# The first two units' queries go from their sums straight into the rows of the max products, and a cleared tile goes

## The chip, the cores and the metric

The kernel runs on one NeuronCore of a Trainium2 chip. The core has five engines, each with a queue of its own that it works through in order: TensorE (PE in the profile; its weight loads are PEld), VectorE (DVE), ScalarE (ACT), GpSimd (POOL) and SyncE (SP), which here only issues transfers. The metric is the device time of one execution in microseconds (us); lower is better.

## The reference

One transformer layer, in float32: 2048 rows of 512, 32 heads of 16 with one shared key and value head, and a GELU MLP of width 1376. The vector `c` gives six rows that shift, scale and gate both halves.

```python
mod = (silu(c) @ w_mod).reshape(1, 6, 1, -1)
sa, ca, ga, sb, cb, gb = (mod[:, i] for i in range(6))
h = layernorm(x) * (1 + ca) + sa
q, k, v = heads(h @ wq), h @ wk, h @ wv
p = softmax(q @ k.T * 16 ** -0.5)
x = x + ga * ((p @ v) @ wo)
h = layernorm(x) * (1 + cb) + sb
x = x + gb * (gelu(h @ w1 + b1) @ w2 + b2)
```

## The kernel before

**Numbers in two parts.** A product is made of three matmuls: each operand is split into a rounded high part and a low part (what the rounding left), and high x high, low x high and high x low are summed in PSUM. `split` makes the two parts, one instruction for each.

**Units.** Attention is made in 64 units: 8 blocks of 256 rows (`HQ`) times 8 groups of four heads. A unit's queries lie in one of four tiles `qst` (`qbufs`), 128 partitions x 2 x 256. In each half of 64 partitions, rows 0 to 15 hold the low part of a head's queries, 16 to 47 the high part twice, and 48 and 49 the row maxima in two parts. `ks` holds the keys in the matching order, with -1 in the rows of the maxima, so one matmul over 64 partitions gives the score minus the maximum. Each unit needs its **max products** first (m, line 517: 32 matmuls, each with one reduction on VectorE, line 522), then its maxima are turned and sent into rows 48 and 49 (`put_max`, line 538), and then come the **score products** (e, 597), the exponentials on ScalarE (p, 598) and the **value products** (acc, 609).

**Queries through DRAM.** `qproj` (before the loop) and `qproj_late` (in the loop) make the queries of 512 rows for a group of two units' heads; `send_q` (413) writes both parts to DRAM, and `load_q` (475) reads them back in the layout of `qst`, four transfers for each of the first four units, six for later ones. The projection for rows 0 to 511 of group 0 serves units 0 and 1, and units 8 and 9.

**Ahead of the loop** the order of every engine's queue is written out by hand. `tc.manual_schedule` keeps each engine's instructions in program order. From line 1259: statistics and normalisation of block 0 of 512 rows (`stats1`, `xhat1`), preparation of the key weights and of the first 128 columns of wq (`prep_wkv`, `prep_wq(0)`), the rows of the modulation (`mod_rows`, `mods`), transposes and scaling of block 0 (`turn1`, `mod1`), and then the first query group, its trip through DRAM for units 0 and 1, the keys and values of block 0, the statistics of blocks 2 and 3 with `heads(1)` among them, and both blocks' normalisation on ScalarE. Then a table, `SLOTS` (line 25), gives the rest: in each slot so many max products (`chunk`), and then named steps, such as "keys 1" (one contraction step of the keys and values of block 1, three matmuls; the last step also copies them out with `kv_out`), "low 1" and "k 1" (the low part of these keys, and its copy for the second half of partitions), "heads 2" (transposes, scaling and splitting of one column block of row block 2), "v 1" (turning the values), "q 1" (a step of the second query group), "wq 1" (weights of a query group), "load" (`load_q` of unit 2) and "rows" (the four late modulation rows). `FIRST_MAX` gives the order of the first 64 max products: units 0 and 1 on each block of 512 keys; the 17th and 18th are the first on block 1. In all 56 max products stand ahead of the loop, two of them in the `while` behind the slots.

Transposes, value transposes, and later the score products share three PSUM banks in turn (`ebank`, e0 to e2); max products have three banks of their own.

**The loop** has 256 bodies, four for each unit. A body makes 8 max products, 8 score products and the 32 value products, and takes one batch of other matmuls if a job offers one, each matmul as two halves over 64 partitions. The jobs in order are the late query projections, the late modulation, more projections, and then the rest of each block (output projection and MLP). A projection is 12 matmuls; `Q_SIZES` cuts it into two batches of 6, or, from job number `Q_LIGHT` on, three of 4. One body in four clock steps; `later(n, fn)` emits a step n clock steps on. Beside that, one step of the weights' preparation stands at the end of a body (`prep_w1`, then `prep_wo`, then `prep_w2`, lines 1082 to 1152): SP loads a piece, and POOL works on it two steps later. `heed` and `wait_early` (462, 467) put the wait for a query transfer on a value product a few clock steps after its issue.

In `prep_w2` the last of 11 pieces has 96 rows of 128; POOL clears the whole tile ahead of its load (1137).

Of the kernel before, what the change touches and what calls it, by code (L numbers as in the profile page):

```python
# [14 lines left out]
P = 128  # L15
# [9 lines left out]
SLOTS = ((4, "keys 1", "keys 1"), (2, "keys 1", "keys 1"), (2, "low 1", "heads 2"), (2, "heads 2", "k 1"), (2, "heads 2"), (2, "heads 2", "v 0"),  # L25
# [10 lines left out]
Q_LIGHT = 12  # L36
# [16 lines left out]
def adaln_mqa_mlp(  # L53
# [282 lines left out]

    hts = {}
# [18 lines left out]
    def xhat1(b, eng):  # L356
# [3 lines left out]
        for t in range(QT):  # L360
# [25 lines left out]

    def kv_out(b):
        ps = kps[b]
        cols = slice(b * BQ, (b + 1) * BQ)
        vt = pro.tile([P, BQ], F32, name=f"vt{b}", tag="vt", bufs=2)  # L390
        for r in range(2):
            nc.scalar.copy(ks[64 * r:64 * r + 48, cols], ps[64 * r:64 * r + 48, :])
        nc.scalar.copy(vt[32:64, :], ps[32:64, :])
        vts[b] = vt

    def low_k(b):
        cols = slice(b * BQ, (b + 1) * BQ)
        nc.vector.tensor_tensor(out=ks[32:48, cols], in0=kps.pop(b)[32:48, :], in1=raw(ks[32:48, cols]), op=ALU.subtract)

# [31 lines left out]
    def qproj(b, g):  # L431

        ps = psum.tile([P, BQ], F32, name=f"qps{b}_{g}", tag="v" if g else "x")
        yield from mm3(ps, qpairs(b, g), 3, 1)
        qH, qL = qtiles(b, g)
        if g == 0:
            nc.scalar.copy(qH, ps)
            nc.vector.tensor_tensor(out=qL, in0=ps, in1=raw(qH), op=ALU.subtract)
        else:
            q32 = pro.tile([P, BQ], F32, name=f"q32_{b}_{g}", tag="h32", bufs=4)  # L440
            nc.scalar.copy(q32, ps)
            split(qH, qL, q32, act, pool)
# [686 lines left out]
    def prep_w2():  # L1129
# [3 lines left out]
        def load(f):  # L1133
            fw = min(P, F - f * P)
            wf = wfs[f] = rp.tile([P, D], F32, name=f"w2f{f}", tag="wf", bufs=3)
            if fw < P:
                nc.gpsimd.memset(wf, 0.0)
            nc.sync.dma_start(out=wf[:fw], in_=w2[f * P:f * P + fw, :])

        def work(f):  # L1140
# [3 lines left out]
            nc.gpsimd.tensor_tensor(out=wfs[f], in0=wfs[f], in1=gb, op=ALU.mult)  # L1144
            split(w2s[g][0][:, f % KD, :], w2s[g][1][:, f % KD, :], wfs[f], nc.gpsimd, nc.gpsimd)
# [65 lines left out]
    projections = [qproj(b, g) for b in range(2) for g in range(KD)]  # L1211
# [50 lines left out]
    prep_wq(0)  # L1262
# [5 lines left out]
    mods()  # L1268
    turn1(0, 2)
# [233 lines left out]
```

## Time and profile before

| | us |
|---|---|
| median of three runs | 1587.57 |
| lowest and highest | 1587.23, 1592.81 |
| the profiled execution's own time | 1589.15 |
| its span, first to last instruction | 1587.3 |

| engine | busy, us | share of the span |
|---|---|---|
| PE | 1562.7 | 98% |
| DVE | 1406.0 | 89% |
| ACT | 1204.3 | 76% |
| POOL | 692.8 | 44% |

A line of a group or of the order of time has the start and the length in us, the engine and line, the operation, what it writes and reads, the shape, how many instructions were merged (x), and in brackets the engine's idle time before it with what ended it, as far as the profile can tell. Matmuls are pipelined, so the lengths of two in sequence overlap; the pace is read from start to start. A line of a window has each engine's busy time and its count of instructions in that stretch, then the granted TensorE clock (PEclk, 1.00 is full), the busy share of the DMA engines and GB/s.

### The profile page before, as it was taken

Reading aid. Unit: us, or ns where it says so; the run is one execution under the profiler, and the core shown is the slowest. Engines: PE = TensorE matmul, PEld = TensorE weight load, DVE = VectorE, ACT = ScalarE, POOL = GpSimd, SP = SyncE. Lnnn points to the kernel's source line nnn. Section 1 sums busy time; section 2 is a strip of 40 time slices with the busy share of each in tenths; the row PEclk is TensorE's granted clock in tenths of the full one; section 3 lists DMA queues with packets and bytes.
Section 4 is the critical chain, followed back from the end, with each engine's and each line's share of the span. In section 5 each row is a group of like instructions: output and inputs, shape, how many; then the busy total and the mean of one; then the engine's idle time right before and its main releaser. Section 6 shows DMA issues by size and latency. Waiting matters only on the chain.

```text
span 1587.3 us, 43409 instructions
## 1 busy us (share of the span) xinstructions
PE 1562.7 (98%) x17491; PEld 1043.9 (66%) x17491; DVE 1406.0 (89%) x2491; ACT 1204.3 (76%) x2417; POOL 692.8 (44%) x1242
## 2 busy tenths in 40 slices
PE   5999999999999999999999999999999999999999
PEld 3556655567766676666766676666766677676667
DVE  6889999899999998999999999999999999999715
ACT  5477777778877887778877887778877788778853
POOL 4345447446513472345622464334712465324721
PEclk8899999999999999999999999999999999999999
DMA  7135423312012120212112130212112130121231
GB/s 263 67 108 177 141 70 101 100 33 97 32 56 67 56 86 23 90 35 94 46 40 86 44 99 19 70 54 86 56 32 92 35 108 22 60 72 50 94 139 68
DMA packets 81022, 121.74 MB, mean 77 GB/s; under 512 B 15966, under 2 KB 55646, under 8 KB 80564
## 3 DMA queue, kind: packets, MB, share of 16 engines
q1 hardware_dynamic: 80804, 118.95, 22.6%
q8 instruction: 137, 2.24, 0.6%
q14 instruction: 65, 0.53, 0.1%
q10 hardware_dynamic: 16, 0.00, 0.0%
HBM read 91.13 MB, written 27.27 MB: 75 GB/s over the span
## 4 chain that ended last, share of the span: by engine, by line
PE 94%; ACT 3%; DVE 1%; DMA 1%; issue 0%; SPq 0%; POOL 0%; DVEq 0%; ACTq 0%
PE acc L609 32%; PE e L597 19%; PE m L517 19%; PE w1ps L193 8%; PE w2ps L193 6%; PE wops L193 3%; PE qps L193 2%; ACT p L598 2%; PE w2ps L187 2%; PE w1ps L187 1%; DVE mx L522 1%; PE tp L193 1%; PE kps L164 1%; PE tp L371 0%; PE modr L289 0%; DMA wm<-in_w_mod_dram 0%
## 5 line engine op out<-in xcount | busy, mean ns | idle before, releaser
L522 DVE TENSOR_REDUCE mx<-m 128x1 f32<-128x512 f32 x2048 | 1271.6, 681 | 105.6 <-PE m L517 95.6
L598 ACT ACTIVATE p<-e 128x512 f32<-128x512 f32 x2048 | 1066.6, 601 | 290.5 <-PE e L597 198.9
L517 PE MATMUL m<-ks,qst 64*128 64x512 f32 x2048 | 829.4, 433 | 6.4 <-DVE ve L205 4.9
L597 PE MATMUL e<-qst,ks 64*128 64x512 f32 x2048 | 729.5, 411 | 2.0 <-ACT wqH L334 1.3
L609 PE MATMUL acc<-p,va 128*32 128x256 f32 x8192 | 550.2, 385 | 1.7 <-DMA qst<-dq 1.7
L517 PEld LDWEIGHTS m<-ks,qst 64*128 64x128 f32 x2048 | 367.4, 184 | 104.6 <-DVE mx L522 85.7
L597 PEld LDWEIGHTS e<-qst,ks 64*128 64x128 f32 x2048 | 356.9, 184 | 112.6 <-ACT p L598 102.6
L609 PEld LDWEIGHTS acc<-p,va 128*32 128x32 f32 x8192 | 214.6, 109 | 219.6 <-issue 113.3
L193 PE MATMUL w1ps<-h2H,w1t 64*128 64x256 f32 x1232 | 236.6, 288 | 0.0
L193 PEld LDWEIGHTS w1ps<-h2H,w1t 64*128 64x128 f32 x1232 | 184.0, 185 | 31.7 <-issue 22.2
L566 POOL TENSOR_SCALAR mt<-turned 8x32 f32<-8x32 f32 x256 | 53.5, 209 | 342.7 <-DVE turned L572 330.6
L193 PE MATMUL w1ps<-h2L,w1t 64*128 64x256 f32 x616 | 169.5, 275 | 0.0
L193 PE MATMUL w2ps<-w2H,gH 64*128 64x256 f32 (+1 forms) x546 | 161.0, 295 | 0.0
L193 PE MATMUL w2ps<-w2H,gL 64*128 64x256 f32 (+1 forms) x546 | 153.9, 282 | 0.0
L193 PE MATMUL w2ps<-w2L,gH 64*128 64x256 f32 (+1 forms) x546 | 153.4, 281 | 0.0
L193 PEld LDWEIGHTS w1ps<-h2L,w1t 64*128 64x128 f32 x616 | 113.7, 185 | 0.0
L193 PEld LDWEIGHTS w2ps<-w2H,gH 64*128 64x128 f32 x546 | 100.5, 184 | 11.7 <-issue 5.4
L193 PEld LDWEIGHTS w2ps<-w2H,gL 64*128 64x128 f32 x546 | 100.7, 184 | 1.7
L193 PEld LDWEIGHTS w2ps<-w2L,gH 64*128 64x128 f32 x546 | 100.7, 184 | 1.3
L949 POOL TENSOR_SCALAR tt<-tt 128x256 f32<-128x256 f32 x77 | 31.2, 406 | 143.8 <-ACT tt L948 143.8
L193 PE MATMUL wops<-woH,onH 64*128 64x256 f32 x224 | 67.9, 303 | 0.0
L193 PE MATMUL wops<-woL,onH 64*128 64x256 f32 x224 | 62.2, 278 | 0.0
(220 smaller groups left out, 1613.1 us busy)
## 6 DMA issues: line engine op xcount, KB each, us to landing
w1t<-dw SPq DMA_DIRECT2D x82, 512.0 KB
qst<-dq SPq DMA_DIRECT2D x128, 64.0 KB
do<-oc SPq DMA_DIRECT2D x64, 128.0 KB
dw<-w1s SPq DMA_DIRECT2D x11, 512.0 KB
xt<-in_A_x_dram SPq DMA_DIRECT2D x4, 1024.0 KB
dq<-qH SPq DMA_DIRECT2D x16, 256.0 KB
dq<-qL SPq DMA_DIRECT2D x16, 256.0 KB
qst<-dq SPq DMA_DIRECT2D x128, 32.0 KB
```

The lines of the kernel that those rows point to most:

```text
L164: nc.tensor.matmul(ps, a, b_, start=begin and n == 0, stop=end and n == last)
L187: nc.tensor.matmul(ps, a, b_, start=first_, stop=last_)
L193: nc.tensor.matmul(ps, a[rows], b_[rows], start=first_ and s == 0, stop=last_ and s == 1)
L517: nc.tensor.matmul(m, qsts[u][rows, j, t * P:(t + 1) * P], ks[rows, kc * 512:(kc + 1) * 512], start=True, stop=True)
L522: nc.vector.tensor_reduce(out=self.mx[u][:, i, kc:kc + 1], in_=m, axis=AX.X, op=ALU.max)
L566: nc.gpsimd.tensor_scalar(out=mt[:, g:g + 32], in0=turned[g:g + 4 * T, :], scalar1=1.0, scalar2=0.0, op0=ALU.mult, op1=ALU.add)
L597: nc.tensor.matmul(e, ks[rows, kt * P:(kt + 1) * P], rhs, start=True, stop=True)
L598: nc.scalar.activation(ptiles[u, K][:, j, s, :], e, AF.Exp, scale=0.25)
L609: ins = nc.tensor.matmul(accs[u][32 * cidx:32 * cidx + 32, :], va[:, kt, :], rhs, start=kt == 0, stop=kt == NKT - 1)
L949: nc.gpsimd.tensor_scalar(out=tt, in0=tt, scalar1=1.0, scalar2=1.0, op0=ALU.mult, op1=ALU.add)
```

## The change

Unit 0's and unit 1's queries no longer go through DRAM ahead of the loop. `prep_w0(u)` makes a weight of 128 columns for each j (two per unit), with the 16 columns of a head repeated three times and 16 columns of zeros, in high and low part: eight parts in all for both units on ScalarE and POOL. `first_queries(u, k)` sums with it into a PSUM bank in the layout of `qst` itself, 24 matmuls of 256 columns for a unit; `queries_out` copies the bank into `qst` (ScalarE), and `low_queries` writes the low part over 16 rows of each half (VectorE). `first_keys` interleaves the keys of block 0 with unit 0's queries, and `low_keys` makes both halves' low parts from PSUM. Unit 0's first two max products stand among unit 1's query products; two and four more follow before `stats1(3)`, and the slots hold 48 instead of 54, so 56 stand ahead of the loop as before. The tail of block 1's normalisation (tiles 2 and 3) is moved to VectorE. The statistics of block 3 come after the eight first max products, where they came ahead of all of them.

The projection of group 0 for rows 0 to 511 becomes the first job of the loop (units 8 and 9 need it), so `prep_wq(0)` moves to a slot near the end, with "wq 2" and "wq 3"; `Q_LIGHT` becomes 14.

In `prep_w2` the tile of the last piece isn't cleared ahead of its load; POOL works on its 96 rows alone, and clears rows 96 to 127 of both parts after that.

```diff
-SLOTS = ((4, "keys 1", "keys 1"), (2, "keys 1", "keys 1"), (2, "low 1", "heads 2"), (2, "heads 2", "k 1"), (2, "heads 2"), (2, "heads 2", "v 0"),
-         (2, "heads 3"), (2, "heads 3"), (2, "heads 3"), (2, "heads 3"), (0, "keys 2"), (2, "keys 2"), (2, "keys 2"), (2, "keys 2"),
-         (2, "low 2", "k 2", "v 1", "wq 1"), (0, "keys 3"), (2, "keys 3"), (2, "keys 3"), (2, "keys 3"), (2, "low 3", "k 3"),
+SLOTS = ((2, "keys 1", "keys 1"), (2, "keys 1", "keys 1"), (2, "low 1", "heads 2"), (2, "heads 2", "k 1"), (2, "heads 2"), (2, "heads 2", "v 0"),
+         (2, "heads 3"), (2, "heads 3"), (2, "heads 3"), (2, "heads 3"), (0, "keys 2"), (1, "keys 2"), (1, "keys 2"), (1, "keys 2"),
+         (1, "low 2", "k 2", "v 1", "wq 1"), (0, "keys 3"), (2, "keys 3"), (2, "keys 3"), (2, "keys 3"), (2, "low 3", "k 3"),
          (0, "v 2"), (2, "q 1"), (2, "q 1"), (2, "q 1"),
-         (2, "q 1", "rows"), (2, "v 3", "load", "wq 2", "wq 3"), (2, "rows"), (2, "rows"), (2, "rows"))
+         (2, "q 1", "rows"), (2, "v 3", "load", "wq 0", "wq 2", "wq 3"), (2, "rows"), (2, "rows"), (2, "rows"))
...
-Q_LIGHT = 12
+Q_LIGHT = 14
+    def prep_w0(u):
+        if u:
+            place_w0(u)
+        for j in range(2):
+            for s in range(2):
+                at = 64 * u + 32 * s + 16 * j
+                w = wqf[:, :, at:at + 16].unsqueeze(2).to_broadcast([P, KD, 3, 16])
+                dh, dl = (t[:, :, j, 64 * s:64 * s + 48].rearrange("p k (o r) -> p k o r", r=16) for t in w0s[u])
+                nc.scalar.copy(dh, w)
+                nc.gpsimd.tensor_tensor(out=dl, in0=w, in1=raw(dh), op=ALU.subtract)
+    def first_queries(u, k):
+        if k == 0:
+            qps[u] = psum.tile([P, 2, HQ], F32, name=f"q0ps{u}", **(ebank() if u else dict(tag="x")))
+        hH, hL = hts[0]
+        wH, wL = w0s[u]
+        for n, (w, h) in enumerate(((wH, hH), (wL, hH), (wH, hL))):
+            for j in range(2):
+                nc.tensor.matmul(qps[u][:, j, :], w[:, k, j, :], h[:, k, 0:HQ], start=k + n + j == 0,
+                                 stop=k == KD - 1 and n + j == 3)
+    def queries_out(u):
+        qsts[u] = qbufs[u]
+        nc.scalar.copy(qbufs[u], qps[u])
+    def low_queries(u, s):
+        rows = slice(64 * s, 64 * s + 16)
+        nc.vector.tensor_tensor(out=qbufs[u][rows], in0=qps[u][rows], in1=raw(qbufs[u][rows]), op=ALU.subtract)
...
-            if fw < P:
-                nc.gpsimd.memset(wf, 0.0)
             nc.sync.dma_start(out=wf[:fw], in_=w2[f * P:f * P + fw, :])
...
+            if fw < P:
+                for t in w2s[g]:
+                    nc.gpsimd.memset(raw(t[fw:, f % KD, :]), 0.0)
...
-    prep_wq(0)
+    prep_w0(0)
...
     mods()
+    prep_w0(1)
     turn1(0, 2)
...
-    rows = xhat1(1, act)
-    run(rows, 2)
-
-    def first_q(t):
+    run(xhat1(1, act, range(2)))
+    run(xhat1(1, dve, range(2, QT)))
+    for k in range(KD):
+        first_queries(0, k)
+        first_keys(k)
+    h1 = heads(1)
+
+    def first_maxima(t):
         if t == 1:
-            run(q_group())
-            load_q(0)
-            load_q(1)
-
-    stats1(2, first_q)
-    run(rows)
-    run(keys(0))
-    low_k(0)
+            queries_out(0)
+            kv_out(0)
+            for s in range(2):
+                low_queries(0, s)
+                low_keys(s)
+            run(h1, 1)
+            first_queries(1, 0)
+            first_queries(1, 1)
+            chunk(1)
+            run(h1, 1)
+            first_queries(1, 2)
+            chunk(1)
+            first_queries(1, 3)
+            values_out(0)
+            kps.pop(0)
+
+    stats1(2, first_maxima)
+    run(h1, 1)
+    queries_out(1)
+    chunk(2)
+    low_queries(1, 0)
+    low_queries(1, 1)
     load_mods(0)
     load_mods(1)
-    h1 = heads(1)
-    run(h1, 2)
-
-    def last_h(t):
-        if t == QT - 1:
-            run(h1)
-
-    stats1(3, last_h)
+    run(h1)
+    chunk(4)
+    stats1(3)
     load_mods(2)
-    repeat_k(0)
     run(xhat1(2, act))
     run(xhat1(3, act))
...
-    late = late[len(late) - len(projections):]
+    late = late[:1] + late[len(late) - len(projections):]
```

More of the change, by code (lines that the diff above doesn't have):

```diff
@@ L335, in prep_wq, with place_w0 @@
             nc.gpsimd.tensor_tensor(out=dl, in0=src, in1=raw(dh), op=ALU.subtract)
+    w0s = []
+    def place_w0(u):
+        place = dict(tag="wm", bufs=4) if u else {}
+        w0s.append([pro.tile([P, KD, 2, P], F32R, name=f"w0{p_}{u}", **place) for p_ in "HL"])
+        for w0 in w0s[u]:
+            for s in range(2):
+                nc.gpsimd.memset(raw(w0[:, :, :, 64 * s + 48:64 * s + 64]), 0.0)
+    place_w0(0)
+    def prep_w0(u):
[8 more added lines that the diff above has]
+                nc.gpsimd.tensor_tensor(out=dl, in0=w, in1=raw(dh), op=ALU.subtract)
     hts = {}
@@ L354, in stats1, with xhat1 @@
         hts_stats[b] = mv, rs, nm
-    def xhat1(b, eng):
+    def xhat1(b, eng, tiles=range(QT)):
         mv, rs, nm = hts_stats[b]
         xt = xts[b]
-        for t in range(QT):
+        for t in tiles:
             if eng is nc.scalar:
@@ L385, in kv_products, with first_keys @@
         return mm3(kps[b], [(wkH[:, k, :], wkL[:, k, :], hH[:, k, :], hL[:, k, :]) for k in range(KD)], 3)
+    qps = {}
+    def first_queries(u, k):
[7 more added lines that the diff above has]
+                                 stop=k == KD - 1 and n + j == 3)
+    def first_keys(k):
+        if k == 0:
+            kps[0] = psum.tile([P, BQ], F32, name="kps0", tag="v")
+        hH, hL = hts[0]
+        for n, (w, h) in enumerate(((wkH, hH), (wkL, hH), (wkH, hL))):
+            nc.tensor.matmul(kps[0], w[:, k, :], h[:, k, :], start=k + n == 0, stop=k == KD - 1 and n == 2)
+    def queries_out(u):
[4 more added lines that the diff above has]
+        nc.vector.tensor_tensor(out=qbufs[u][rows], in0=qps[u][rows], in1=raw(qbufs[u][rows]), op=ALU.subtract)
     def kv_out(b):
@@ L398, in low_k, with low_keys @@
         nc.vector.tensor_tensor(out=ks[32:48, cols], in0=kps.pop(b)[32:48, :], in1=raw(ks[32:48, cols]), op=ALU.subtract)
+    def low_keys(s):
+        nc.vector.tensor_tensor(out=ks[64 * s + 32:64 * s + 48, 0:BQ], in0=kps[0][64 * s + 32:64 * s + 48, :],
+                                in1=raw(ks[64 * s + 32:64 * s + 48, 0:BQ]), op=ALU.subtract)
     def repeat_k(b):
@@ L431, in qproj @@
     def qproj(b, g):
-        ps = psum.tile([P, BQ], F32, name=f"qps{b}_{g}", tag="v" if g else "x")
+        ps = psum.tile([P, BQ], F32, name=f"qps{b}_{g}", tag="v")
         yield from mm3(ps, qpairs(b, g), 3, 1)
         qH, qL = qtiles(b, g)
[L436 to L442, printed above, removed]
+        q32 = pro.tile([P, BQ], F32, name=f"q32_{b}_{g}", tag="h32", bufs=4)
+        nc.scalar.copy(q32, ps)
+        split(qH, qL, q32, act, pool)
         send_q(b, g, qH, qL)
@@ L1210, in adaln_mqa_mlp @@
     late = [qproj_late(b, g) for b in range(2) for g in range(KD)]
-    projections = [qproj(b, g) for b in range(2) for g in range(KD)]
+    projections = [qproj(b, g) for b in range(2) for g in range(KD)][1:]
     def project(n):
```

15 lines of the change are left out of this document (10 added, 5 removed).

## The prediction

> **What bounds the kernel now.** I read the table of time windows first, to split the run into the stretch ahead of the loop and the loop itself, and inside the loop one row for each kind of loop body.
>
> ```profile
> core 0 of [0], span 1587.3 us
> core 0: us, PE busy (x) PEld busy (x) DVE busy (x) ACT busy (x) POOL busy (x), PEclk, DMA share, GB/s
> 47.70:57.70 10.00, 10.00 (x32) 5.70 (x30) 6.33 (x11) 6.23 (x10) 8.54 (x8) 0.50 0.31 107
> 93.29:202.52 109.23, 109.23 (x1143) 68.81 (x1141) 100.47 (x170) 81.81 (x158) 53.73 (x77) 1.00 0.46 151
> 202.52:269.26 66.74, 66.74 (x675) 38.68 (x673) 62.26 (x106) 51.23 (x100) 40.76 (x53) 1.00 0.25 84
> 269.26:284.92 15.66, 15.45 (x145) 7.78 (x145) 15.48 (x29) 12.26 (x25) 13.31 (x18) 1.00 0.25 76
> 284.92:293.21 8.29, 6.61 (x49) 3.03 (x48) 4.96 (x9) 4.50 (x11) 3.77 (x7) 1.00 0.33 101
> ```
>
> A loop body holds 8 max products, 8 score products and 32 value products, 48 matmuls; with a batch of six projection products in halves it has 60, with four it has 56. So the four loop rows are 19 bodies of 60 (1143), 12 of 56 (675), three of 48 (145) and one of 48 (49). A body costs 109.23/19 = 5.75 us, 66.74/12 = 5.56 and 15.66/3 = 5.22. The last one takes 8.29 with the same work. In the loop TensorE is covered to the last microsecond, so the loop gains only by fewer products or by losing such a stall. The first row lies ahead of the loop: TensorE is busy for all of it, but at half its clock.
>
> Then the order of time on each engine, ahead of the loop. TensorE:
>
> ```profile
> 33.45 1.19 PE L517 MATMUL m<-ks,qst 64*128 64x512 f32 x3 [4.90 <-DVE ve L205]
> ...
> 51.64 1.12 PE L371 MATMUL tp<-ident,xt 128*128 128x128 f32 x4
> 52.69 0.80 PE L517 MATMUL m<-ks,qst 64*128 64x512 f32 x2
> 53.41 1.11 PE L371 MATMUL tp<-ident,xt 128*128 128x128 f32 x4
> 54.18 0.77 PE L164 MATMUL kps<-big2H,wkH 128*128 128x512 f32 x1
> ```
>
> The first max product comes after 4.90 us of idle: that is the trip of the queries through DRAM. The later rows are the pace of the slots that turn blocks 2 and 3: a pair of max products 0.72 (52.69 to 53.41), the four transposes of one head 1.05 (51.64 to 52.69), 1.77 together. The keys of block 2 start at 54.18. ScalarE and VectorE in the same stretch:
>
> ```profile
> 32.48 5.75 ACT L362 ACTIVATE xt<-xt,nm,rs 128x512 f32<-128x512 f32 x8
> 41.56 1.17 ACT L392 CAST ks<-kps 48x512 fp32r<-48x512 f32 x2 [3.33 <-PE kps L164]
> 42.74 0.58 ACT L393 COPY vt<-kps 32x512 f32<-32x512 f32 x1
> 43.35 0.78 ACT L377 ACTIVATE h<-tp,sa,ca 128x512 f32<-128x512 f32 x1
> 44.16 0.62 ACT L134 CAST big2H<-h 128x512 fp32r<-128x512 f32 x1
> ```
> ```profile
> 27.07 0.68 DVE L398 TENSOR_TENSOR ks<-kps,ks 16x512 fp32r<-16x512 f32 x1 [0.71 <-ACT vt L393]
> 27.78 2.48 DVE L199 BATCH_NORM_STATS2 st<-xt 128x6 f32<-128x512 f32 x4
> ...
> 32.81 0.36 DVE L203 BATCH_NORM_AGGREGATE mv<-st 128x2 f32<-128x6 f32 x4
> 33.21 0.17 DVE L205 TENSOR_SCALAR ve<-mv 128x4 f32<-128x4 f32 x1
> 34.25 2.48 DVE L522 TENSOR_REDUCE mx<-m 128x1 f32<-128x512 f32 x4 [0.87 <-PE m L517]
> ```
>
> What to see: the statistics of block 3 (the x4 at 27.78, ending in ve at 33.21) are made while the queries travel. So ScalarE normalises blocks 2 and 3 in one piece (the x8 at 32.48) and is free when the keys of block 1 are done, at 41.56. The idle 4.90 us of TensorE are used by the others.
>
> **The change part by part.** First the start. ScalarE and POOL make the first weight pieces in eight parts of 128x192 instead of two of 128x256.
>
> ```profile
> 13.96 1.55 POOL L335 TENSOR_TENSOR wqL<-wqf,wqH 128x256 fp32r<-128x256 f32 x2 [2.90 <-ACT wqH L334]
> 17.90 1.29 POOL L139 TENSOR_TENSOR h0L<-h,h0H 128x512 fp32r<-128x512 f32 x1 [2.39 <-ACT h0H L134]
> 19.16 0.62 POOL L132 TENSOR_SCALAR h0H<-h 128x512 fp32r<-128x512 f32 x1
> 19.74 1.02 POOL L207 TENSOR_TENSOR rs<-ve,mhalf 128x4 f32<-128x4 f32 x1
> ```
>
> The subtractions are POOL's: 0.78 each today, so 0.58 for three quarters of the elements (estimate by size). Eight of them and the four small clearings between (0.7, an estimate from the 0.54 of a 128x512 clearing, quoted below) run from 13.9 to 19.2, and h0L, now at 17.90, starts 1.3 later. The ends: 0.4 each would hide in the 2.39 of idle before h0L, 1.29 each (the 512-element row) would cost 5.7 more. ScalarE's copies lie in waits of its own and cost about 0.1. TensorE has the same 24 full products' worth up to the first keys (24 of half length for the two-sided queries, 12 for the keys), and catches up part of the 1.3: I take 0.6. Today the keys are done 1.75 ahead of 27.07 (three copies: 1.17 and 0.58), at 25.3; then 25.9, and the queries, one key step earlier, at 25.2. Copying them out takes 0.5, then VectorE makes four low parts of 0.68: done at 28.5. The first reduction moves from 34.25 to 28.5. That is the gain, 5.7 at this place.
>
> Second, what now stands in VectorE's queue ahead of the statistics of block 3. From 28.5: four reductions (0.62 each, 2.48), 0.6 for the second max product, which stands behind unit 1's first query products, two statistics of block 2 (1.24), their sums and ve (0.53), one low half of block 1 (0.68), two low query parts (1.36): 35.4. Only then is the PSUM bank of unit 1's queries free, which the last transposes of block 1 take. Those (half of 1.05), h (0.78) and its cast (0.62) take 2.0 in which VectorE waits; then the low half 0.68, four reductions 2.48, the statistics of block 3 2.48 and 0.53: 43.7, where ve is at 33.21 now. POOL's rs (1.02) and two small steps (0.5) make it 45.3. ScalarE has four of the eight normalisations behind that (2.9, half of 5.75): 48.2. And behind these stands the copying of the keys of block 1, today at 41.56: 6.6 later. This is the wait that takes the place of the one removed: ScalarE, in order, for block 3's statistics. Eight more maxima are reduced by then than today at this step, but ScalarE, not VectorE, is what is late.
>
> Third, its heirs. The first h of block 2 starts at 49.95 (43.35 now); with cast (1.35), the next h (0.8) and the repeated keys (0.6) it is 52.7. The 18th max product needs these repeated keys; it now stands in the fifth slot where it stood in the eighth, so TensorE waits for them. From 52.7, at half clock: one max product 0.36, transposes 1.05, a slot 1.77 with small value transposes 0.4, four slots of 1.77: 63.4 for the keys of block 2, 54.18 now, 9.2 later. Why half clock: in the first window row the clock is 0.50 through these same slots, and TensorE has less to do before them. From there on six max products fewer stand ahead of the loop: three at 0.36 and three at about half of that, with the clock back, 1.7 off. That leaves 7.5. At the end ScalarE has four more pieces:
>
> ```profile
> 81.23 1.34 ACT L334 CAST wqH<-wqf 128x256 fp32r<-128x256 f32 x4
> 82.46 0.58 ACT L1319 COPY modl_sb<-modl 128x512 f32<-128x512 f32 x1
> 83.19 1.58 ACT L598 ACTIVATE p<-e 128x512 f32<-128x512 f32 x3
> ```
>
> Two more copies of wq (0.67) and the two of the last queries (0.58, 0.62) now stand behind unit 0's maxima, 1.9 before the first p; but one set of modulation products and the end of a query group come behind them too. Between 0 and 1.9 I take 0.2. The sum ahead of the loop is +7.7. Its ends: -5.7, if the early start went through whole, and +13.4 with POOL's dear price.
>
> Fourth, the loop. Units 8 and 9 still need the first group's queries for rows 256 to 511, so one projection more is made in the loop: 15 jobs for 14. With Q_LIGHT at 14 thirteen of them take two bodies and two take three, 32 bodies as before: six bodies turn from four products to six. 6 x (5.75 - 5.56) = +1.1. The batches of later work begin in the same bodies, since w1's own preparation is what holds up wo and w2. The transfers of these queries go through DRAM long before unit 8.
>
> Fifth, w2's last piece.
>
> ```profile
> 276.58 1.29 POOL L139 TENSOR_TENSOR w2L<-w2f,w2H 128x512 fp32r<-128x512 f32 x1
> ...
> 281.13 0.54 POOL L1137 MEMSET w2f<- 128x512 f32 x1
> ```
> ```profile
> 281.69 0.34 SPq L1138 DMA_DIRECT2D w2f<-in_B_w_dram  x1
> ...
> 286.23 0.61 SPq L487 DMA_DIRECT2D qst<-dq  x1
> ```
> ```profile
> 289.00 0.62 PE L609 MATMUL acc<-p,va 128*32 128x256 f32 x2 [0.85 <-DMA qst<-dq]
> 290.44 0.83 PE L609 MATMUL acc<-p,va 128*32 128x256 f32 x9 [0.82 <-DMA qst<-dq]
> ```
>
> SP issues the load of w2's last piece only when POOL's clearing ends (281.67), and everything behind it on SP waits: the sums, the outputs, and at 286.23 the queries of a later unit, for which TensorE then stands. The buffer itself was free at 277.87. Without the clearing SP goes on 3.8 sooner, the wait of TensorE in the body of 8.29 is covered, and it is a body of 5.22: -3.1 (ends: 0 and -3.1). The two clearings of 32 rows that come instead are behind POOL's other work; if they were in the open they would cost 1.1 (two of 0.54).
>
> The sum: 7.7 + 1.1 - 3.1 = +5.7. The profiled execution took 1589.15 (span 1587.3 and 1.85 around it), so 1594.9 for its like; it is 1.6 above the median of the runs, 1587.57, so the forecast is **1593.3**. That is 0.36% slower, within the 0.5% (7.9 us) that a measurement of this kernel can tell from no change.
>
> **The rivals.** *Full clock in the slots* (0.12). If the clock comes back once TensorE is busy without a gap, the slots run at VectorE's pace, two reductions of 0.62 instead of 1.77 for TensorE: six slots save 3.1 and the keys 1.1, so 1589.1. Against it: 10.00 of 10.00 busy at clock 0.50 in the window row. [...]
>
> *The early start goes through* (0.17). If ScalarE is not held up by block 3's statistics, because other work fills it, the first reduction's 5.7 last to the loop: -5.7 + 1.1 - 3.1 = -7.7, 1579.9. For it: VectorE has 34.25 as its first reduction today and 56 of them to do before the loop. Against it: an engine's queue is in order, and rows 32.48 and 41.56 show ScalarE using the wait that goes.
>
> *POOL's pieces are dear* (0.15), the one that ends slower. Eight pieces, with sources read three times over, at 1.29 as the 512-element row instead of 0.58: h0L, rs and all behind it come 5.7 later, 1599.0. It decides (over 1595.5) from 0.28 more for each piece. Against it: the 128x256 row at 0.78, nearer in size.
>
> *The w2 edit does nothing* (0.06). If the load still waits, for its buffer behind later POOL work, the stall stays: 1596.4.
>
> **How the numbers follow.** The forecast has 0.5, the rivals what stands beside them. Over 0.5% faster (under 1579.7) is about a third of the second rival, 0.06. Over 0.5% slower (over 1595.5) is most of the third and the fourth (0.16 of their 0.21) and 0.09 of the forecast's 0.5, whose own spread over a dozen rounded steps is some 2.5 us: 0.25. The rest, 0.69, is within 0.5%. The range reaches into the second and the third rival and leaves out a tenth on each side: 1581 to 1598.
>
> **What would show it.** In the changed profile: the first reduction at about 28.5; ve of block 3 near 43.7 and a hole of some 5 us on ScalarE before its last four normalisations; the clock at 0.5 through the slots of blocks 2 and 3; the keys of block 2 starting near 63; the first p near 91 instead of 83.19; 26 bodies of 5.75 and six of 5.56; no body of 8.29, and the last w2 load not behind POOL. The prediction is wrong if the copying of block 1's keys comes before 45, if the first p comes before 86, or if h0L starts later than 21.

## The result, and the profile after

The changed kernel takes 1603.78 us (median of four runs, 1601.5 to 1605.64), the kernel before beside it 1587.4 (1585.86 to 1592.81). The ratio is 1.0096 with an interval of 1.0069 to 1.0124: slower by 1.0%, where 1593.3 was forecast and the range ended at 1598. Its profiled execution took 1603.18 (span 1601.3). Against the profiled execution of before (1589.15) that is 14.0 more. The medians differ by 16.4, since before's profiled execution lay 1.75 above its median and after's 0.6 below. One execution of e11 below, of seven, took 2381.38 us at a mean granted clock of 0.558; the ratios leave it out, and the median given for e11 (1593.37) too.

In these two executions all 14.0 us lie ahead of the loop: the first p, the first exponential of the loop's scores, comes at 97.21 instead of 83.19, and from there to the end both kernels take 1504.1. The table of windows of the kernel after shows both halves. The first three rows run from the first key product of block 2 to the last of block 3, from there to the reduction that completes unit 0's maxima, and from there to the first p. Then come 25 loop bodies of 60 matmuls, six of 56, one of 48 and one body more.

```profile
core 0: us, PE busy (x) PEld busy (x) DVE busy (x) ACT busy (x) POOL busy (x), PEclk, DMA share, GB/s
64.75:77.44 12.69, 11.66 (x42) 6.07 (x40) 7.57 (x13) 4.80 (x10) 4.22 (x7) 0.95 0.00 1
77.44:89.67 12.23, 10.45 (x27) 5.18 (x26) 7.59 (x12) 2.56 (x5) 0.00 (x0) 0.59 0.00 0
89.67:97.21 7.54, 7.22 (x47) 2.06 (x46) 5.46 (x10) 3.56 (x11) 3.85 (x9) 0.99 0.11 42
...
107.42:251.14 143.72, 143.72 (x1502) 90.17 (x1500) 132.43 (x225) 107.35 (x207) 68.70 (x101) 1.00 0.40 133
251.14:284.52 33.38, 33.38 (x338) 19.37 (x336) 31.02 (x52) 25.86 (x51) 24.32 (x28) 1.00 0.33 99
300.20:305.59 5.39, 5.39 (x49) 2.78 (x48) 4.96 (x9) 4.50 (x11) 3.21 (x6) 1.00 0.38 123
...
322.28:330.56 8.28, 7.90 (x75) 4.50 (x73) 5.63 (x11) 4.47 (x10) 0.00 (x0) 1.00 0.38 127
```

The second row is the news: 12.23 us at a clock of 0.59, with TensorE busy for 10.45. The same stage of before is the second row here, in the table of windows of the kernel before:

```profile
54.18:66.69 12.51, 12.51 (x46) 6.52 (x44) 9.81 (x17) 5.11 (x10) 3.99 (x4) 0.86 0.00 1
66.69:76.85 10.16, 9.85 (x46) 4.63 (x50) 8.74 (x14) 3.77 (x7) 1.35 (x4) 1.00 0.07 24
76.85:83.19 6.34, 5.00 (x34) 1.51 (x31) 5.34 (x10) 1.92 (x6) 3.16 (x11) 1.00 0.16 57
```

Three stages, 29.01 us before and 32.46 after, though the changed kernel reduces fewer maxima in them. The loop rows are as forecast (143.72/25 = 5.75 a body, 33.38/6 = 5.56), and the body of 8.29 is 5.39 now; but another of 8.28 has come four bodies later.

Then the order of time on the engines of the kernel after, beside the lines of before that the prediction shows. TensorE, where it waits:

```profile
36.10 1.09 PE L395 MATMUL tp<-ident,xt 128*128 128x128 f32 x4 [4.39 <-DVE qst L439]
...
51.80 0.50 PE L575 MATMUL m<-ks,qst 64*128 64x512 f32 x1 [2.03 <-DVE ks L456]
53.86 0.79 PE L575 MATMUL m<-ks,qst 64*128 64x512 f32 x1 [1.55 <-ACT ks L464]
...
72.75 0.49 PE L575 MATMUL m<-ks,qst 64*128 64x512 f32 x1 [0.88 <-DVE ks L456]
...
80.01 1.44 PE L575 MATMUL m<-ks,qst 64*128 64x512 f32 x2 [1.78 <-DVE ks L456]
```

ScalarE and VectorE:

```profile
46.45 2.93 ACT L386 ACTIVATE xt<-xt,nm,rs 128x512 f32<-128x512 f32 x4 [4.96 <-POOL nm L377]
49.29 1.16 ACT L445 CAST ks<-kps 48x512 fp32r<-48x512 f32 x2
50.45 0.58 ACT L451 COPY vt<-kps 32x512 f32<-32x512 f32 x1
51.06 0.78 ACT L401 ACTIVATE h<-tp,sa,ca 128x512 f32<-128x512 f32 x1
```
```profile
29.12 0.69 DVE L580 TENSOR_REDUCE mx<-m 128x1 f32<-128x512 f32 x1
...
34.59 1.37 DVE L439 TENSOR_TENSOR qst<-q0ps,qst 16x512 fp32r<-16x512 f32 x2
...
41.81 2.46 DVE L199 BATCH_NORM_STATS2 st<-xt 128x6 f32<-128x512 f32 x4
44.19 0.36 DVE L203 BATCH_NORM_AGGREGATE mv<-st 128x2 f32<-128x6 f32 x4
44.59 0.17 DVE L205 TENSOR_SCALAR ve<-mv 128x4 f32<-128x4 f32 x1
```

The forecast chain is there nearly row for row: the early reduction (29.12), the late statistics (ve ends at 44.76), the hole of 4.96 us on ScalarE, the late copy of the keys of block 1 (49.29). The four lower rows of TensorE are max products that wait for keys just made. The prediction had the one at 53.86, the 18th max product, which it let wait until 52.7 for the repeated keys of block 1 (the row at 51.80 is the product ahead of it). It did not have those at 72.75 and 80.01, which wait for the keys of blocks 2 and 3.

In the loop, POOL (and SP, TensorE below it) around the new body of 8.28:

```profile
311.33 1.28 POOL L1201 TENSOR_TENSOR w2f<-w2f,gb 128x512 f32<-128x512 f32 x1
...
314.65 1.29 POOL L1201 TENSOR_TENSOR w2f<-w2f,gb 96x512 f32<-96x512 f32 x1
...
318.07 0.52 POOL L1205 MEMSET w2H<- 32x512 f32 x1
318.53 0.52 POOL L1205 MEMSET w2L<- 32x512 f32 x1
319.12 1.02 POOL L624 TENSOR_SCALAR mt<-turned 8x32 f32<-8x32 f32 x4
```
```profile
320.54 0.64 SPq L619 DMA_DIRECT2D qst<-mh  x1
...
323.19 0.63 SPq L545 DMA_DIRECT2D qst<-dq  x1
```
```profile
322.28 2.58 PE L667 MATMUL acc<-p,va 128*32 128x256 f32 x16
```

Two pieces of w2 (7.8 us from 311.33 to 319.12) stand on POOL ahead of a unit's turned maxima. SP sends these maxima at 320.54 and only behind them loads the next unit's queries, and the value products that carry that wait take 2.58 us.

### The profile page after: what moved, and what is told of

Same layout as the page of the kernel before. It is cut to its first block, busy times and chain, and to the rows that moved or that the text cites. A ratio compares the mean times of both kernels' runs of the same rounds, so it can differ in the third digit from the quotient of the medians.

```text
span 1601.3 us, 43556 instructions
## 1 busy us (share of the span) xinstructions
PE 1572.9 (98%) x17551; PEld 1051.1 (66%) x17551; DVE 1412.3 (88%) x2498; ACT 1204.8 (75%) x2423; POOL 698.7 (44%) x1261
## 4 chain that ended last, share of the span: by engine, by line
PE 91%; ACT 3%; POOL 2%; DMA 1%; DVE 1%; issue 1%; SPq 1%; POOLq 0%; DVEq 0%
PE acc L667 31%; PE e L655 18%; PE m L575 18%; PE w1ps L193 8%; PE w2ps L193 6%; PE wops L193 3%; PE qps L193 2%; ACT p L656 2%; PE w2ps L187 2%; PE w1ps L187 1%; PE tp L193 1%; DMA wqf<-in_A_wq_dram 1%; PE tp L395 1%; DMA qst<-dq 0%; DVE mx L580 0%
```

## The experiments

Each kernel is the kernel after with the edit shown, unless said otherwise. The table has, from each kernel's profiled execution, the start of the keys of block 2, the time from the last key product of block 3 to the first p, the first p, and the rest of the span; then the median and the ratio to the kernel before that ran beside it. The times of a stage are those of one execution; medians of kernels that ran beside different runs of before (whose medians were 1586.1 to 1587.8) are best compared by their ratios. The *q slots* are the four slots with a step of the second query group, "q 1".

| kernel | keys 2 start | last key product to first p | first p | rest | median | ratio (interval) |
|---|---|---|---|---|---|---|
| before | 54.18 | 16.5 | 83.19 | 1504.1 | 1587.4 | |
| after | 64.75 | 19.8 | 97.21 | 1504.1 | 1603.78 | 1.0096 (1.0069 to 1.0124) |
| e1 statistics first | 61.49 | 20.1 | 96.67 | 1504.6 | 1603.77 | 1.0109 (1.0094 to 1.0124) |
| e2 normalised in slots | 65.45 | 19.6 | 100.76 | 1504.5 | 1606.73 | 1.0124 (1.0109 to 1.014) |
| e3 two maxima later | 64.56 | 19.4 | 94.53 | 1506.2 | 1600.21 | 1.0091 (1.0077 to 1.0105) |
| e4 before, w2's edit alone | 50.73 | 16.5 | 78.21 | 1501.5 | 1581.71 | 0.9973 (0.9962 to 0.9984) |
| e5 w2 on time | 64.72 | 19.8 | 97.05 | 1501.4 | 1600.72 | 1.0086 (1.007 to 1.0102) |
| e6 cleared early | 64.36 | 18.0 | 94.81 | 1504.4 | 1601.88 | 1.0102 (1.0083 to 1.0122) |
| e7 = e1 + e3 + e5 | 62.75 | 16.6 | 90.63 | 1502.7 | 1596.69 | 1.0054 (1.0041 to 1.0066) |
| e8 filled | 66.27 | 16.6 | 97.88 | 1505.5 | 1604.92 | 1.0105 (1.0086 to 1.0123) |
| e9 = e4, filled | 50.14 | 19.4 | 80.51 | 1500.2 | 1580.07 | 0.9955 (0.994 to 0.997) |
| e10 = e5, filled | 61.59 | 16.8 | 90.53 | 1504.5 | 1597.61 | 1.006 (1.0047 to 1.0072) |
| e11 = e7, filled | 61.03 | 17.3 | 88.79 | 1504.1 | 1593.37 | 1.0033 (1.002 to 1.0045) |
| e12 filled late | 63.24 | 16.6 | 91.94 | 1504.7 | 1601.0 | 1.0103 (1.0086 to 1.0121) |

**e1: block 3's statistics ahead of the last transposes of block 1.**

```diff
+    stats1(3)
     run(h1)
     chunk(4)
-    stats1(3)
```

> The changed kernel with one line moved: the statistics of block 3 stand ahead of the last transposes of block 1 and the four max products behind them, so VectorE makes them while it now waits 2.73 us for ScalarE. Theory A (ScalarE, in order, is held up by block 3's statistics): ve of block 3 near 39 instead of 44.6, block 1's keys copied out near 44.6 instead of 49.3, the first p 4 to 5 us earlier than 97.2, about 1599. Rival B (what costs is the extra work of the direct sums themselves, 24 half-length products and eight weight pieces): the order of the statistics moves nothing, 1603 to 1604.

The time stays (1603.77), which is rival B's, but the order does move something. ScalarE's order of time in e1 shows the hole gone and who is late then:

```profile
40.67 3.61 ACT L386 ACTIVATE xt<-xt,nm,rs 128x512 f32<-128x512 f32 x5
47.49 1.17 ACT L445 CAST ks<-kps 48x512 fp32r<-48x512 f32 x2 [3.21 <-PE kps L164]
```

The normalisation ends at 44.3, but the keys of block 1 are copied out at 47.49 only, since TensorE has just made them. ScalarE's queue had thus held them up by 49.29 - 47.49 = 1.8 us, not by all of the lateness; the keys of block 2 start 3.3 sooner. And the gain is lost again: the two stages behind take 15.06 and 12.10 us, with two waits for fresh keys of 2.7 together and half clock from 69.7 to 76.5 and from 79.9 to 90.2, and the first p is only 0.5 earlier.

**e2: ScalarE's normalisation of block 3 spread over the slots, behind the copying of the keys.**

```diff
-SLOTS = ((2, "keys 1", "keys 1"), (2, "keys 1", "keys 1"), (2, "low 1", "heads 2"), (2, "heads 2", "k 1"), (2, "heads 2"), (2, "heads 2", "v 0"),
+SLOTS = ((2, "keys 1", "keys 1"), (2, "keys 1", "keys 1"), (2, "low 1", "heads 2"), (2, "heads 2", "k 1", "x 3"), (2, "heads 2", "x 3"), (2, "heads 2", "v 0", "x 3", "x 3"),
...
-    run(xhat1(3, act))
...
```

> The changed kernel with the four normalisations of block 3 moved on ScalarE behind the copying of block 1's keys, into slots 4 to 6; statistics and maxima stay where they are. If the hole of 4.96 us on ScalarE is by itself what the start loses, 4 to 5 us come back. By theory A as the trace has it, block 1's keys are summed only at 47.5, since their products stand behind max products that wait for VectorE: copying out moves from 49.3 to 47.5 at most, and ScalarE gets 2.9 us in the slots instead, so between 1.8 faster and 1 slower.

Slower still, and outside what was expected: 1606.73, first p 100.76 (the interval of its ratio overlaps after's). Nothing on ScalarE stands ahead of the copying now, and it still starts at 48.72, behind a wait of 7.61 us for TensorE's key products. With e1 this says that TensorE is as late as ScalarE by itself, here in a half-clock stretch of 13.7 us from 36.5. The four normalisations come back in the slots, where ScalarE has no room for them (the keys of block 2 start 0.7 later, and the two blocks' keys take 15.70 us with 2.7 us of waits for fresh keys).

**e3: two of the maxima of the slots of block 2's keys moved behind the slots.**

```diff
-         (2, "heads 3"), (2, "heads 3"), (2, "heads 3"), (2, "heads 3"), (0, "keys 2"), (1, "keys 2"), (1, "keys 2"), (1, "keys 2"),
-         (1, "low 2", "k 2", "v 1", "wq 1"), (0, "keys 3"), (2, "keys 3"), (2, "keys 3"), (2, "keys 3"), (2, "low 3", "k 3"),
+         (2, "heads 3"), (2, "heads 3"), (2, "heads 3"), (2, "heads 3"), (0, "keys 2"), (1, "keys 2"), (1, "keys 2"), (0, "keys 2"),
+         (0, "low 2", "k 2", "v 1", "wq 1"), (0, "keys 3"), (2, "keys 3"), (2, "keys 3"), (2, "keys 3"), (2, "low 3", "k 3"),
```

> The changed kernel with two max products fewer ahead of the low parts of block 2's keys (the table has 1, 1, 0, 0 in the slots of block 2's keys), and two more at the end, so the first products on blocks 2 and 3 come a slot after their keys, as in the kernel before. Theory C (the 14 us ahead of the loop, where 7.7 were forecast, hold a second loss: max products that wait for keys just made, which then bring a second stretch at half clock): TensorE's waits at 72.75, 73.40 and 80.01 (2.8 us) go, the clock stays full from 79 to 89, 4 to 6 us faster. Rival: the second stretch comes from the thin work of these slots by itself, and the result stays within 1.5 us.

The waits for fresh keys of blocks 2 and 3 are gone: the stage of the two blocks' keys takes 10.56 us instead of 12.69, and the first p comes 2.7 earlier. Of these 2.1 us some 0.8 are the two products themselves (0.42 each, shown further down), which now stand behind the slots. But the clock does not stay full, as the theory had it: the next stage takes 13.02 us at 0.74, with half clock from 78.7 to 85.5. So the waits alone do not make the half clock over the q slots. Of the 2.7 the rest of the span gives 2.1 back: its first body takes 7.54 us (6.56 in after), the stalled one 9.64 (8.28).

**e4: the kernel before with w2's edit alone.** The hunk of `prep_w2` shown with the change, and nothing else.

> The kernel before with the edit of w2's last piece alone. Theory D (the edit removes the stall; that it came back four bodies later is the work of the shifted schedule): the body of 8.29 us becomes one of 5.3, none of 8 us comes after it, 2.5 to 3 us faster than before. Rival (the two clearings of 32 rows, 0.52 us each, delay POOL's turned maxima and so bring the stall back by themselves): within 0.7 us of before, with a body over 7 us four bodies later.

1581.71, faster by 0.27%. No body but the first takes over 6.2 us; the rest of the span is 1501.5 against 1504.1. So this half of the change does what was forecast: 2.6 against 3.1. The medians beside each other differ by more, 4.8 us, and the first p of this execution lies 5.0 ahead of before's, though the instructions ahead of the loop are the same: this execution has one half-clock stretch of 10.2 us there, before's has two.

**e5: w2's preparation a body earlier.** It is started once the late modulation is seen to be done, which is looked at only when a projection job ends. With `Q_LIGHT` at 14 the jobs end in other bodies, and it starts one body later than in the kernel before.

```diff
-            if state["mods"] and "w2" not in preps:
+            if "wo" not in weights and "w2" not in preps:
```

> The kernel after, with one condition changed: w2's preparation starts once wo is in the weights, not when the modulation is seen to be done at the end of a projection job, so that it starts one body earlier, in the body in which the kernel before starts it. Theory (the stall of 8.28 us at body 39 is POOL working on w2 while the turned maxima wait, since with lighter batches the jobs end later and the preparation starts late): the body of over 8 us is gone, the loop from the first p goes from 1504.1 to about 1501.5, time 1601.2 (1600 to 1602). Rival (the stall comes of the two new clearings of 0.52 us or of the lighter batches themselves): body 39 stays over 8 us, time 1603.8 as the kernel after.

As the theory has it: the rest of the span is 1501.4, no body but the first over 6.1 us, 1600.72. It is the trace that shows this, with the same half-clock stretches as after; the intervals of the two ratios overlap. POOL in e5 has one piece ahead of the turned maxima, not two:

```profile
310.72 1.27 POOL L1201 TENSOR_TENSOR w2f<-w2f,gb 96x512 f32<-96x512 f32 x1
...
314.58 0.52 POOL L1205 MEMSET w2L<- 32x512 f32 x1
315.17 1.02 POOL L624 TENSOR_SCALAR mt<-turned 8x32 f32<-8x32 f32 x4
```

**e6: the two clearings of 32 rows moved away from that place**, to where the tiles are placed. The start stays late.

```diff
+                if NF - f <= KD:
+                    for t in w2s[g]:
+                        nc.gpsimd.memset(raw(t[F % P:, (NF - 1) % KD, :]), 0.0)
...
-            if fw < P:
-                for t in w2s[g]:
-                    nc.gpsimd.memset(raw(t[fw:, f % KD, :]), 0.0)
```

> The kernel after, with the 32-row clearing of w2's last piece (two of 0.52 us on POOL) moved from behind the last piece's own work to the moment at which its tiles are placed, two pieces earlier; the start of w2's preparation stays late. Theory (the late start makes the stall): the turned maxima wait for two pieces as before, only about 1.0 us less, body 39 stays at 7.2 to 8.3 us, time 1602.8 to 1603.8. Rival (the new place of the clearing makes the stall): body 39 falls to about 5.7, time 1601.2.

The stalled body is 7.89 us, 0.4 shorter, and the rest of the span 1504.4: the clearings are not the cause, the late start is. The median, 1601.88, lies below the expected 1602.8 to 1603.8; its runs spread from 1601.06 to 1607.44 with the granted clock from 0.984 to 0.991, so no more is read into it. Its first p is worth a look: 94.81 against 97.21, though nothing is changed ahead of the loop. The waits for fresh keys are the same to 0.02 us (0.88, 0.15 and 1.78), but the half clock over the q slots lasts 3.4 us here and 10.2 in after.

**e8: products that nobody reads, in TensorE's gaps.** 128 x 512 into a free PSUM bank, to see what the half clock costs.

```diff
+    def fill(n, **place):
+        ps = psum.tile([P, BQ], F32, name=f"fill{len(idles)}", **(place or dict(tag="x")))
+        idles.append(ps)
+        for _ in range(n):
+            nc.tensor.matmul(ps, wkH[:, 0, :], wkH.rearrange("p k n -> p (k n)"), start=True, stop=True)
...
     stats1(2, first_maxima)
+    fill(12)
     run(h1, 1)
...
-    for n, *names in SLOTS:
+    for i, (n, *names) in enumerate(SLOTS):
+        if i in (3, 4):
+            fill(6)
+        if i == 21:
+            fill(8, **ebank())
         chunk(n)
```

> The kernel after, with products that nobody reads (128 x 512, into a free bank) on TensorE where it has gaps ahead of the loop: 12 ahead of the third transposes of block 1, 6 ahead of the maxima of the fourth and the fifth slot, 8 ahead of the first slot of the query products. They take about 0.23 us each at the full clock, and stand where the trace of after shows TensorE idle for 4.4, 2.0, 1.6 and 1.8 us. Theory (half of the excess of the prologue over the forecast is half clock): the half-clock stretches shrink from 10.2 + 13.7 + 10.2 us to at most one of 10.2, the four q slots go from 2.3 to about 1.35 us each (-3.8), the keys of block 2 start at about 62 instead of 64.75, the first p comes at 90 to 92 instead of 97.2, time 1597 to 1599. Rival (the order of the work alone sets the slots, the clock is hidden behind reductions and ScalarE): the clock is full but the first p stays within 1 us of 97.2, time 1603 to 1605; up to +3 more if the fillers stand in the way.

By its time the rival holds: 1604.92, first p 97.88. The stages say that it isn't so simple. The first 12 products stood ahead of transposes that were ready, not in the gap: ve of block 3 is 3.1 later (47.88), the keys of block 2 start 1.5 later. But from the last key product to the first p it takes 16.6 us instead of 19.8, at full clock. What it wins there it loses ahead of it (1.5, and 2.4 more in the stage of the two blocks' keys, at half clock from 59.2 to 69.4 and from 76.3 to 79.7), so that this run decides nothing by its total.

**e10: the filling in the right places, on e5.** 18 behind the two maxima that follow `queries_out(1)`, 6, 6 and 4 ahead of slots 3 to 5, 4 and 8 ahead of slots 16 and 21 (counted from 0).

> The kernel after with w2's preparation a body earlier, and products that nobody reads in TensorE's own gaps, the first lot now behind the two maxima that follow block 0's second unit, where the 4.4 us of idle time are (in e8 it stood ahead of transposes that were ready, and moved them by 3.1 us): 18 there, 6, 6 and 4 ahead of the slots in which the keys of block 1 are waited for, 4 and 8 ahead of the first maxima of the keys of blocks 2 and 3. Theory (half clock costs about 4 us in the q slots and 2 to 3 in the slots of heads and keys): granted clock 0.996 or more, the four q slots 1.35 us each, first p at 90 to 92 against 97.05, time 1594 to 1596.5. Rival (order alone sets the slots): clock full, first p within 1.5 us of 97, time 1600 to 1603.

The half clock ahead of the loop is one stretch of 6.8 us, where e5 has 10.2, 13.7 and 10.2. The first p comes at 90.53 instead of 97.05, inside the expected 90 to 92: with the order of the work untouched, 6.5 us were the clock, in one execution beside one (e6 differs from after by 2.4 with no such products). The time, 1597.61, is 1.1 over the expected end, since 3.1 are given back in the loop: its first body runs at half clock now (8.35 us against 6.27), and another takes 6.54.

**e12: only the last of these products, on the kernel after.** 4 ahead of slot 16 and 8 ahead of slot 21; nothing is changed ahead of 70 us.

> The kernel after, with only the last of the products that nobody reads: 4 ahead of the first maxima of block 2's keys, 8 ahead of the first maxima of block 3's, where TensorE waits for these keys (0.88 and 1.78 us); nothing is changed ahead of 72 us. Theory (these waits bring the half clock of the q slots, and that stretch alone is 3.2 us of the excess): the last keys end as in after, near 77.4; from there to the first p 16.5 to 16.8 us at full clock instead of 19.77, first p at 94, time about 1600.5 (1599.5 to 1601.5). Rival (the stretch of 19.77 us is set by the late keys themselves): it stays at 19 or more, first p within 0.5 of 97.2, time 1603.8.

The stages of e12, in the same three windows as above:

```profile
63.24:75.40 12.16, 12.00 (x47) 6.47 (x45) 7.85 (x13) 5.09 (x10) 5.13 (x8) 1.00 0.00 1
75.40:84.41 9.01, 9.01 (x42) 4.87 (x42) 7.55 (x12) 2.56 (x5) 0.00 (x0) 1.00 0.00 0
84.41:91.94 7.53, 6.56 (x46) 1.90 (x38) 5.46 (x10) 3.56 (x10) 3.84 (x9) 1.00 0.11 42
```

The second stage takes 9.01 us at 1.00, where after has 12.23 at 0.59: 3.2 us from twelve products that are thrown away. They make no key earlier; they stand in the place of the waits. So it is not the late keys that set this stage, but the clock. That the waits of 0.88 and 1.78 us alone bring it down is not shown: e3 and e9 have half clock there without them. The profiled execution's first p is another 2.0 us early, 1.5 of it because the keys of block 2 start at 63.24; nothing was changed there, and its half-clock stretches lay otherwise (33.9 for 17.1 us, 54.3 for 6.8). In the total the gain is not clear of noise: the median is 1601.0 against after's 1603.78, but beside their own runs of before the ratios are 1.0103 and 1.0096, and the profiled execution (1598.54) is the fastest of the four.

**e7: the three edits of e1, e3 and e5 together.**

> The kernel after with three edits together: block 3's statistics ahead of the last transposes of block 1 (as e1), two of the maxima of the slots of block 2's keys later (as e3), and w2's preparation a body earlier (as e5). Theory (e1's 3.3 us were lost behind keys waited for, which e3 takes away): now both reach the first p, 97.2 - 3.3 - 2.7 = 91.2; the loop as e3 less the stall, about 1503.6; time about 1597 (1595.5 to 1598.5). Rival (the half clock sets the slots, so that gains ahead of it are lost again): first p at 94 to 95, as e3 alone, time 1598.5 to 1601.

1596.69, as the theory has it, with the first p at 90.63 and 16.6 us for the last stages at full clock. e1 and e3 alone moved the first p by 0.5 and 2.7, together by 6.6. Part of that is the clock: e3's execution has 6.8 us of half clock over the q slots and e7's none, so the 6.6 is not the order's alone.

**e11: e7 with the products of e10.**

> The three edits of e7 with the products of e10 that nobody reads. Theory (order and clock are separate costs): first p 5 to 6 us ahead of e7's, 86 to 89, time 1591 to 1594, still 3 to 7 us over the kernel before, since block 2's keys start about 6 us later than there. Rival (the clock is full without the fillers once nothing is waited for): within 1.5 us of e7.

1593.37, inside the expected 1591 to 1594. The first p is only 1.8 earlier than in e7 (88.79), not 5 to 6, so order and clock are not separate costs: e7's execution already has no half clock over the q slots, which is one of the stretches that the products are there to remove. And it is still slower than before, by 0.33%.

**e9: e4 with 22 such products behind the last transposes of block 1.**

```diff
             run(h1)
+            fill(22)
```

> The kernel before with w2's edit alone (1581.7), and 22 products that nobody reads behind the last transposes of block 1, where TensorE is idle for 4.9 us. Theory: the half-clock stretch of 10.2 us over the keys of block 1 (12 products of 0.63 and 0.4 us) goes; these keys end 1.5 to 3 us earlier; the slots behind are held by the reductions (1.25 us per two), so 1 to 2 us reach the first p, 78.2 to 76.5 or 77; time 1579.5 to 1581. Rival (keys of block 1 wait for ScalarE and the reductions in any case, or the gate falls in a later stretch instead): first p within 0.5 us of 78 or as late as 83, time 1581.5 to 1586.

1580.07, the fastest kernel here: ratio 0.9955 (0.994 to 0.997) to the kernel before, against 0.9973 for w2's edit alone, so the two intervals still overlap. The time is in the theory's range. Its profiled execution is the slowest of its runs, with the first p at 80.51, later than the theory's 76.5 to 77: the half clock over the keys of block 1 is gone, but a stretch of 6.8 us lies over the q slots instead. The stage behind the last key product so shows the same price without the change ahead of the loop. First e9, then e4:

```profile
61.14:74.17 13.03, 12.71 (x46) 5.91 (x50) 8.73 (x14) 3.77 (x7) 1.47 (x4) 0.74 0.06 21
```
```profile
61.71:71.86 10.15, 9.84 (x47) 4.63 (x50) 8.75 (x14) 3.77 (x7) 1.34 (x4) 1.00 0.06 23
```

The same work of TensorE (46 and 47 records), 13.03 us with the clock at 0.74 and 10.15 at 1.00.

## Why the prediction was wrong, point by point

**POOL's eight pieces: right.** They follow each other at 0.60 and 0.56 us (0.58 forecast); h0L starts at 19.00, 1.1 later, not 1.3. The rival that had them dear falls.

**The early start: right.** The first reduction comes at 29.12, forecast 28.5, from 34.25.

**What takes its place: right in the order and nearly in the numbers.** ve of block 3 at 44.76 (43.7), the hole of 4.96 (some 5), the copying at 49.29 (48.2), the keys of block 2 at 64.75 (63.4). These are 10.6 us later where 9.2 were forecast. The step "ScalarE, not VectorE, is what is late" names one of two: by e1 and e2 ScalarE's queue is worth 1.8 us at this place, and TensorE, slowed by the same wait of VectorE's and by half clock, has the keys ready only at 47.5. The second rival, the early start that goes through, falls with it.

**From the keys of block 2 to the first p: wrong, and the larger miss.** The prediction took 1.7 off "with the clock back" for six maxima fewer, and added 0.2 for ScalarE. In place of -1.5 the profiled executions show +3.4 (29.01 to 32.46). Three things in this step failed.

The maxima were priced by the product, 0.36 and half of that. But a lone max product holds TensorE as long as a pair. TensorE of after, at full clock:

```profile
67.47 0.49 PE L575 MATMUL m<-ks,qst 64*128 64x512 f32 x1
67.89 0.50 PE L164 MATMUL kps<-big2H,wkH 128*128 128x512 f32 x1
...
74.72 0.49 PE L575 MATMUL m<-ks,qst 64*128 64x512 f32 x2
75.14 0.51 PE L164 MATMUL kps<-big3H,wkH 128*128 128x512 f32 x1
```

From the start of the lone product to the next instruction it is 0.42 us (67.47 to 67.89), and for the pair 0.42 too (74.72 to 75.14). At half clock the lone product at 53.86 takes 0.72 to the next instruction, where the prediction had 0.36. Four of the six leave a product alone in its slot and save TensorE nothing; only the pair behind the slots is saved, so 0.4 in place of 1.7.

The waits for fresh keys were not in the sum. Eight maxima stand ahead of the slots, so the first max products on new keys stand right behind the step that makes these keys, and TensorE waits (0.88, 0.15 and 1.78 us); e3 takes these waits away. With both, and at full clock, the three stages take 28.70 us in the new order (e12, whose thrown-away products stand in the waits) and 27.48 in the old (10.98, 10.15 and 6.35 in e4): +1.2.

And the clock did not come back for good: a stretch of 10.2 us at half clock lies over the q slots, where before's execution has none. e12 prices it at 3.2 us, e9 beside e4 at 2.9; at full clock the last two stages take 16.5 us in either order (before 10.16 and 6.34, e12 9.01 and 7.53). With 0.5 more in the first stage (12.69 in after, 12.16 in e12), less the 1.5 that before's own half clock cost in its first stage (12.51 against 10.98 in e4), 1.2 + 3.2 + 0.5 - 1.5 is the 3.4. What brings this stretch stays open. The waits alone do not settle it: with the same waits it is 10.2 us in after and 3.4 in e6, and without them 6.8 in e3 and e9 and none in e7. The first rival, full clock in the slots, falls: from 52.3 to 65.9 the granted clock is 0.50 in after.

**The whole term.** +7.7 ahead of the loop was +14.0. e10, with 6.8 us of half clock ahead of it, has the first p at 90.53, where the prediction had it near 91. This agreement is partly luck: before has half-clock stretches too (10.2 and 10.2 us ahead of the loop), and with one of them only, the same instructions bring the first p at 78.21 (e4's execution). With one stretch on each side (6.8 in e10, 10.2 in e4) the change still costs some 12 us there (90.53 - 78.21).

**The loop's bodies: right.** 5.75 and 5.56, in the counts forecast.

**w2: right by itself, then lost.** The old stall is gone as forecast (e4: -2.6). The step that failed is "the batches of later work begin in the same bodies". With three more of the jobs cut in two batches of six, the jobs' ends shift, w2's preparation starts a body later, and two of its pieces meet a unit's maxima on POOL: 8.28 us again. e5 moves the start back and has the 2.7 us. The loop's balance, -2.0 in the forecast, was 0.0.

The misses, 6.3 ahead of the loop and 2.0 in it, are the 8.3 between +5.7 and +14.0. The other 2.2 of the 10.5 between 1593.3 and 1603.78 is not the kernel's: the forecast took 1.6 off because before's profiled execution lay above its median, and after's lies 0.6 below. What stays open is how the clock's share of the median difference divides: executions of one kernel differ with their granted clock (the kernel before in one series: 1584.4 us at 0.996, 1592.0 at 0.990), and no run shows after and before with the same stretches. Nor does a run separate what the extra work of the direct sums costs: e11, with the order, w2's start and the clock mended, is still 0.33% slower than before, and its keys of block 2 start at 61.03.

## What to carry to other kernels

A transfer taken off the critical path also takes away the waiting time in which other engines did their preparation; list what was done in that time and whom its new place holds up. Ahead of a steady loop, where TensorE has gaps, price a stage at full and at half clock: here the same instructions brought the first p at 83.19 or 78.21 and at 97.21 or 94.81, by where the half clock fell, so one execution does not price a wait of one or two microseconds. A product fewer saved TensorE something here only where its partner in the pair went with it: the lone max product took 0.42 us to the next instruction, and the pair 0.42 too. And when a batch size changes, look at every start that is polled at a batch's end: a body's shift of one job can put it ahead of another on a queue that nobody touched.

## What was not expected of the hardware

From 20 us to the loop's first bodies the half-clock stretches of these executions are 3.4, 6.8, 10.2, 13.7 or 17.1 us long: 10.2, 10.2 and 3.4 in before, 10.2, 13.7 and 10.2 in after. Cut into windows of 3.4 us, the kernel after shows where the clock falls and how long it stays down:

```profile
48.90:52.30 3.40, 1.37 (x7) 0.60 (x5) 1.54 (x3) 3.32 (x6) 0.00 (x0) 0.99 0.00 0
52.30:55.70 3.40, 1.84 (x8) 1.08 (x7) 2.06 (x4) 1.48 (x3) 3.05 (x3) 0.50 0.00 0
55.70:59.10 3.40, 3.40 (x14) 2.13 (x15) 1.60 (x3) 2.91 (x5) 1.43 (x3) 0.50 0.25 43
59.10:62.50 3.40, 3.40 (x14) 1.86 (x13) 2.44 (x5) 2.18 (x3) 2.28 (x2) 0.50 0.66 267
62.50:66.00 3.50, 3.50 (x13) 2.28 (x12) 2.40 (x4) 2.18 (x3) 3.11 (x4) 0.51 0.00 0
66.00:69.40 3.40, 3.40 (x11) 1.71 (x11) 1.46 (x3) 0.62 (x1) 1.50 (x2) 1.00 0.02 5
...
76.20:79.60 3.40, 2.03 (x11) 1.02 (x11) 3.24 (x6) 1.74 (x3) 0.00 (x0) 0.99 0.00 0
```

Here a window with 1.37 or 2.03 us of work is followed by half clock; then, behind 52.30, three windows busy from end to end go by at 0.50 before it comes back. But the busy time alone does not decide. In the kernel after a window with 2.57 us of work (69.30 to 72.70) is not followed by half clock, and in e9 one with 3.08 is, and a wholly busy one behind it does not end it:

```profile
61.40:64.80 3.40, 3.08 (x13) 1.54 (x11) 3.24 (x6) 2.34 (x5) 0.00 (x0) 1.00 0.00 0
64.80:68.20 3.40, 3.40 (x8) 1.94 (x8) 2.17 (x5) 0.00 (x0) 0.00 (x0) 0.50 0.02 5
68.20:71.60 3.40, 3.40 (x11) 1.33 (x14) 1.77 (x3) 0.28 (x1) 0.00 (x0) 0.50 0.00 0
```

So one wholly busy window did not bring the full clock back here, neither with transposes and products over 64 rows (55.70 to 62.50 in after, 6.80 us busy at 0.50) nor with query products over 128 rows among them (3.40 of 3.40 us busy at 0.50 from 64.80 in e9, and again from 68.20). Nor do the instructions alone say where the stretches fall: with the same ones ahead of the loop, before has two of 10.2 us there and e4 one, and the first p comes at 83.19 and 78.21; over the q slots after has 10.2 us and e6 3.4, and it comes at 97.21 and 94.81.
